# Twenty-four 64x64 zero products in place of five 128x128 ones at the start of an attention and gated-MLP kernel

## The chip, the core and the metric

One core of one Trainium2 chip runs the whole program. The metric is device microseconds of one execution, from the first to the last instruction of the kernel and what the runtime puts around it. The profile is of one execution, taken by the hardware profiler.

## What is computed

Eight batches of eight heads of linear attention (no softmax), then a gated MLP with a spatial gate, everything in single precision:

```python
kv = np.einsum('bhsd,bhse->bhde', k, v)          # 64x64 for each head
out = np.einsum('bhsd,bhde->bhse', q, kv)
attn = out / np.sqrt(np.mean(out * out, -1, keepdims=True) + 1e-06) * g_norm
x = attn.transpose(0, 2, 1, 3).reshape(8, 576, 512)
h = np.maximum(x @ w_in, 0.0)                    # 512 -> 1024
u, v = h[..., :512], h[..., 512:]
v_n = (v - mean(v)) / np.sqrt(var(v) + 1e-06)
v_s = np.einsum('ts,bsd->btd', w_spatial, v_n) + b_spatial[None, :, None]
return (u * v_s) @ w_out
```

There are 576 positions, heads of 64, and inputs in HBM.

## The kernel before

TensorE does nearly all of the arithmetic. The large products (lines 482, 515, 763) split each operand into a high and a low half of type f32r and use three matmuls for one product. The attention products (line 289 for K'V, line 320 for Q times K'V) work on 64x64 pieces in plain f32. The trace shows a plain f32 product as two matmuls, each with its own weight load, and an f32r product or a transpose as one.

Batch 0 is staged by hand, since weights and inputs arrive while it runs. The string PLAN lists its steps in program order, one token a step. Of the tokens that matter here: `L` issues the next load of keys, values or queries (lines 213 to 223, on SP's queue), `W` the next load of weights, `Kbp` the K'V products of batch b and head pair p (line 289, the result copied to KVB by ScalarE on line 305), `A` the products with Q (line 320), `D` the squares and sums for the norm (lines 365 to 373 on ScalarE, 366 on VectorE, then 232), `B` the scaling (line 390), `T` the transposes (line 425) and their split into X0H and X0L (lines 246, 247), `c` and `C` the decoding of a weight tile (lines 907 on ScalarE, 913 and 914 on VectorE), `X` its split (518, 519), `H` the products of X with the weights. Two buffers hold keys and values, so the third load of them waits for the first K'V products.

Two tokens compute nothing that is used. `N8` calls `warm(8)`, eight 128x128 products of a block of zeros (KVO) into the tile psw, line 1017. `n1` calls `filler(1)`, one such product into psh, line 1021. They keep TensorE busy while the first loads are under way.

The order in which each engine issues its instructions is not the program's. ORDER holds, for each engine, a run-length list: each number says how many of the instructions still left to pass over before the next is taken, and a number after a point how many are taken in a row. The end of the program adds dependencies that hold the scheduler to this order. On TensorE the eight products of `warm` stand in three places: one, then four, then three after the first Q products.

Of the kernel before, what the change touches and what calls it, by code (L numbers as in the profile page):

```python
# [16 lines left out]
B, H, S, D = 8, 8, 576, 64  # L17
# [15 lines left out]
ODD = 32  # L33
NB = B
PLAN = """
L L N8 n1 n1 n1 n1 W G K00 n1 n1 L L W c A00 n1 n1 n1 n1 n1 D00 C X0 B00 K01 L L W T00 c A01 D01 H00 H20 H10 H30 C X1 K02 L L W B01 T01 c A02 D02 H01 H21 H11 H31
C X2 K03 L W W B02 T02 c W A03 D03 H02 H22 H12 H32 C X3 W B03 c T03 W a0 C X4 H03 e0 H23 e2 H33 e3 H13 e1 b0 t0 c u00 C X5
L L K10 f2 F1 c u01 F0 L L W y0 F3 C X6 u02 y2 y1 W c K12 L a1 C X7 u03 b1 Z L L y3 t1 u10 A10 D10 W W E1 L L E0
u11 W z u12 h B10 A12 u13 W s T10 D12 s s s B12 T12 s s s s Y1 Y0 P Q0 O0 Q1 W p O1 R
# [1 line left out]

ORDER = {
    "PE": """
# [97 lines left out]
def body(ctx: ExitStack, tc, qT, qtl, kvm, kvt, g2, w_in, wsT, bsp, w_out, out):  # L141
    nc = tc.nc
# [10 lines left out]
    def persistent(shape, dt, name):  # L153
        return const.tile(shape, dt, name=name, tag=name)
# [36 lines left out]
    KVO = [persistent([P, 2, P], F32, f"KVO{i}") for i in range(2)]  # L191
# [76 lines left out]
    def two_banks(name):  # L268
        ps = ps_att.tile([P, 1024], F32, name=name, tag="att")
        banks = [ps[:, 0:512], ps[:, 512:1024]]  # L270
        whole[id(banks)] = ps
        return banks
# [740 lines left out]
    def warm(n):  # L1013

        ps = two_banks("psw")[0]
        for _ in range(n):
            nc.tensor.matmul(ps[:, 0:P], KVO[1][:, 1], KVO[1][:, 1], start=True, stop=True)

    def filler(n):
        for _ in range(n):  # L1020
            nc.tensor.matmul(psv[3][:, 0:P], KVO[1][:, 1], KVO[1][:, 1], start=True, stop=True)  # L1021
# [47 lines left out]
    def to_out():  # L1069
# [14 lines left out]
    two = lambda b, p: (p, p + 1) if b else (p,)  # L1084
    do = {
        "N": warm, "n": filler,
        "L": lambda: ahead(), "W": lambda: loads.pop(0)(), "c": lambda: weight64_a(makes[0].pop(0)),
        "C": lambda: weight64_b(makes[1].pop(0)),
# [86 lines left out]
    for name, text in ORDER.items():  # L1175
        left, last = queues[getattr(mybir.EngineType, name)], None
        for token in text.split():
            at, n = (int(x) for x in (token + ".1").split(".")[:2])
# [55 lines left out]
```

## Time and profile before

| | us |
|---|---|
| median of 3 runs | 475.3 |
| lowest and highest | 474.8, 475.54 |
| the profiled execution | 475.17 |
| its span, first to last instruction | 473.4 |
| TensorE matmul busy in the span | 465.7 |
| ScalarE busy | 303.2 |
| VectorE busy | 361.7 |

The profiled execution took 475.17 us, of which its span is 473.4; the other 1.8 us lie around the span. In the views, a row with a line number names the engine, the line of the kernel, the operation, the tile written and the tiles read, the shape, and how often. "idle before <-X" is the time in which the engine had nothing to do before the row, and what ended it; "issue" stands where nothing that the profile shows ended it. Matmul ends are modelled, so the distance between starts tells more than the durations.

### The profile page before, as it was taken

To read this page: it belongs to the slowest core of one execution; us is meant where nothing else is said; L and a number is where in the kernel's file an instruction comes from. 1 tells how busy PE (TensorE), PEld (TensorE's weight loads), DVE (VectorE), ACT (ScalarE), POOL (GpSimd) and SP (SyncE) were. 2 spreads that over 40 slices of the span, in tenths; PEclk is the share of its full clock that TensorE was granted. 3 is DMA by queue.
4 is the path that set the end of the run, shared out by engine and by line. 5 is a ranking of instruction groups with operands and counts; after the bars stand their busy time and mean duration, and the time that the engine had idled before them with its cause. 6 is when DMAs were issued, how large, how long until landed. Compare 5 with 4: busy or idle time off the path is not lost.

```text
span 473.4 us, 12500 instructions
## 1 busy us (share of the span) xinstructions
PE 465.7 (98%) x4922; PEld 415.5 (88%) x4922; DVE 361.7 (76%) x1007; ACT 303.2 (64%) x971; POOL 20.9 (4%) x43
## 2 busy tenths in 40 slices
PE   8999999999999999999999999899999999999996
PEld 8679998989888999889988899789998899989995
DVE  2987798876977889778866798579887679878760
ACT  4899967756546866478534886367743688547531
POOL 3000100000001010000000010000000001000000
PEclk9999999999999999999999999999999999999999
DMA  8997227226724931462713817055531344114313
GB/s 272 373 326 242 75 75 247 81 101 182 263 95 121 320 132 48 135 225 93 256 30 91 265 54 289 4 187 178 198 140 56 74 162 140 40 67 157 125 55 111
DMA packets 27763, 72.02 MB, mean 152 GB/s; under 512 B 3508, under 2 KB 8120, under 8 KB 26168
## 3 DMA queue, kind: packets, MB, share of 16 engines
q1 hardware_dynamic: 23880, 48.61, 30.9%
q0 software_dynamic: 3456, 22.02, 13.7%
q8 instruction: 38, 0.62, 0.5%
q10 hardware_dynamic: 368, 0.59, 0.4%
q14 instruction: 21, 0.17, 0.1%
HBM read 58.10 MB, written 13.11 MB: 150 GB/s over the span
## 4 chain that ended last, share of the span: by engine, by line
PE 95%; ACT 3%; issue 1%; DVE 0%; ACTq 0%
PE pso L482 21%; PE psh L515 16%; PE psb L763 10%; PE psub L763 8%; PE psa L763 5%; PE psc L763 5%; PE psuc L763 4%; PE pskv L289 4%; PE pso L320 3%; PE psu L482 3%; PE psu L763 3%; PE psua L763 2%; PE pstr L425 2%; PE psh L482 2%; PE psh L1021 1%; PE psh L763 1%
## 5 line engine op out<-in xcount | busy, mean ns | idle before, releaser
L482 PE MATMUL pso<-WO,G 128*128 128x512 f32 x384 | 110.7, 393 | 0.0
L482 PEld LDWEIGHTS pso<-WO,G 128*128 128x128 f32 x384 | 70.3, 188 | 13.1 <-ACT o L860 0.2
L515 PE MATMUL psh<-WVH,XL 128*128 128x512 f32 x112 | 43.2, 392 | 0.0
L515 PE MATMUL psh<-WVL,XH 128*128 128x512 f32 x112 | 43.1, 391 | 0.0
L515 PE MATMUL psh<-WVH,XH 128*128 128x512 f32 x112 | 43.0, 391 | 0.0
L518 ACT CAST G<-g 128x288 fp32r<-128x288 f32 (+1 forms) x56 | 22.5, 406 | 29.1 <-DVE g L782 29.0
L860 ACT COPY o<-pso 128x512 f32<-128x512 f32 x35 | 20.2, 586 | 26.9 <-PE pso L482 26.4
L494 DVE BATCH_NORM_STATS2 s<-v 128x6 f32<-128x512 f32 x31 | 21.4, 690 | 16.9 <-ACT v L488 16.4
L763 PE MATMUL psb<-WSL,VH 128*128 128x288 f32 x112 | 32.5, 296 | 0.0
L763 PE MATMUL psb<-WSH,VH 128*128 128x288 f32 x112 | 32.2, 299 | 0.0
L763 PE MATMUL psb<-WSH,VL 128*128 128x288 f32 x112 | 32.1, 295 | 0.0
L519 DVE TENSOR_TENSOR VL<-v,VH 128x512 fp32r<-128x512 f32 (+1 forms) x42 | 24.9, 599 | 8.2 <-ACT VH L518 8.1
L488 ACT ACTIVATE v<-psh 128x512 f32<-128x512 f32 x31 | 18.6, 600 | 19.6 <-PE psh L515 19.2
L519 DVE TENSOR_TENSOR G<-g,G 128x288 fp32r<-128x288 f32 (+1 forms) x56 | 23.3, 421 | 8.3 <-ACT G L518 7.5
L502 ACT ACTIVATE v<-v,mv,rv 128x512 f32<-128x512 f32 x28 | 22.6, 815 | 8.1 <-DVE mv L501 7.8
L518 ACT CAST VH<-v 128x512 fp32r<-128x512 f32 (+1 forms) x42 | 22.8, 546 | 4.7 <-DVE v L547 4.2
L515 PEld LDWEIGHTS psh<-WVH,XL 128*128 128x128 f32 x112 | 21.0, 188 | 3.8
L515 PEld LDWEIGHTS psh<-WVL,XH 128*128 128x128 f32 x112 | 21.0, 188 | 3.7
L515 PEld LDWEIGHTS psh<-WVH,XH 128*128 128x128 f32 x112 | 21.0, 188 | 3.7
L246 ACT ACTIVATE XH<-pstr,gcol 128x512 fp32r<-128x512 f32 x28 | 19.2, 689 | 6.3 <-PE pstr L425 3.9
L289 PEld LDWEIGHTS pskv<-KV 64*64 64x64 f32 (+1 forms) x960 | 18.3, 135 | 4.0 <-issue 1.7
L247 DVE SCALAR_TENSOR_TENSOR XL<-pstr,gcol,XH 128x512 fp32r<-128x512 f32 x28 | 20.6, 746 | 1.4 <-ACT XH L246 1.2
(289 smaller groups left out, 1392.7 us busy)
## 6 DMA issues: line engine op xcount, KB each, us to landing
KV<-kvm SPq DMA_DIRECT2D x32, 512.0 KB, 5.7
WO<-spare_o POOLq DMA_DIRECT2D x12, 1024.0 KB, 6.9
UX<-spare_u POOLq DMA_DIRECT2D x12, 768.0 KB, 6.8
qt<-qT SPq DMA_DIRECT2D x32, 256.0 KB, 4.4
out<-o SPq DMA_DIRECT2D x32, 256.0 KB, 3.1
stage<-w_in SPq DMA_DIRECT2D x7, 512.0 KB, 6.8
stage<-w_out SPq DMA_DIRECT2D x4, 512.0 KB, 4.1
spare_o<-WO SPq DMA_DIRECT2D x8, 256.0 KB, 4.0
```

What stands on the lines that cost most here:

```text
L246: nc.scalar.activation(hi, ps, AF.Copy, scale=gcol)
L247: nc.vector.scalar_tensor_tensor(lo, ps, gcol, f32(hi), op0=ALU.mult, op1=ALU.subtract)
L289: return nc.tensor.matmul(banks[r if b else 0][h:h + D, at:at + D], of[own, 0, h:h + D], of[own, 1, h:h + D], start=begin, stop=end)
L482: nc.tensor.matmul(ps, lt, rh, start=i == 0, stop=i == n - 1)
L488: nc.scalar.activation(v, ps, AF.Relu)
L494: nc.vector.bn_stats(s6, v)
L502: nc.scalar.activation(v, v, AF.Identity, bias=m, scale=r)
L515: nc.tensor.matmul(ps, lt, rh, start=k == 0 and i == 0, stop=k == NP - 1 and i == 2)
L518: nc.scalar.copy(hi, x)
L519: nc.vector.tensor_tensor(lo, x, f32(hi), op=ALU.subtract)
L763: nc.tensor.matmul(ps, lt, rh, start=start and i == 0, stop=stop and i == len(pairs) - 1, skip_group_check=True)
L860: nc.scalar.copy(o, ps)
```

## The change

`warm(n)` now issues n products of 128x128 and then 8n products of 64x64 of the same zeros, on rows and columns 0 to 63. PLAN calls it with 3 where it called it with 8. So three large products stay, and 24 small ones stand for the other five.

```diff
-L L N8 n1 n1 n1 n1 W G K00 n1 n1 L L W c A00 n1 n1 n1 n1 n1 D00 C X0 B00 K01 ...
+L L N3 n1 n1 n1 n1 W G K00 n1 n1 L L W c A00 n1 n1 n1 n1 n1 D00 C X0 B00 K01 ...
...
     "PE": """
-8 0 7.3 0.4 13.2 3.10 19 3.16 0.6 1.10 0 8.16 0.8 12.10 0.3 6 0 5 14.16 ...
+27 0 26.3 0.26 10.2 0.10 16 0.19 1.10 0 8.16 0.8 12.10 0.3 6 0 5 14.16 ...
...
         for _ in range(n):
             nc.tensor.matmul(ps[:, 0:P], KVO[1][:, 1], KVO[1][:, 1], start=True, stop=True)
+        for _ in range(8 * n):
+            nc.tensor.matmul(ps[0:D, 0:D], KVO[1][0:D, 1, 0:D], KVO[1][0:D, 1, 0:D], start=True, stop=True)
```

P is 128 and D is 64. The rest of the TensorE list and the lists of the other engines are as they were.

On TensorE, from the first instruction to the Q products of the second head pair, this stood before (psw and psh take the zeros of KVO; pskv takes the attention products of KV, its tail KT, and of the queries qt):

```order
L1021 MATMUL psh<-KVO_102 128x128
L1017 MATMUL psw<-KVO_102 128x128
L1021 MATMUL psh<-KVO_102 128x128 x3
L1017 MATMUL psw<-KVO_102 128x128 x4
L1021 MATMUL psh<-KVO_102 128x128 x2
L289 MATMUL pskv<-KV_103 64x64 x8
L289 MATMUL pskv<-KT_105 64x64 x2
L1021 MATMUL psh<-KVO_102 128x128
L320 MATMUL pskv<-KVB,qt 64x64 x16
L1017 MATMUL psw<-KVO_102 128x128 x3
L1021 MATMUL psh<-KVO_102 128x128 x3
L289 MATMUL pskv<-KV_104 64x64 x8
```

The two added lines make line 1021 line 1023 and put the small products on line 1019. On the same stretch stands now:

```order
L1023 MATMUL psh<-KVO_102 128x128
L1017 MATMUL psw<-KVO_102 128x128
L1023 MATMUL psh<-KVO_102 128x128 x3
L1017 MATMUL psw<-KVO_102 128x128 x2
L1019 MATMUL psw<-KVO_102 64x64 x24
L1023 MATMUL psh<-KVO_102 128x128 x2
L289 MATMUL pskv<-KV_103 64x64 x8
L289 MATMUL pskv<-KT_105 64x64 x2
L1023 MATMUL psh<-KVO_102 128x128
L320 MATMUL pskv<-KVB,qt 64x64 x16
L1023 MATMUL psh<-KVO_102 128x128 x3
L289 MATMUL pskv<-KV_104 64x64 x8
```

All 24 small products stand ahead of the first K'V products, where two large ones went; the three large ones between the first Q products and the second K'V products are gone. From there on TensorE issues the same instructions in the same order as before.

## Rows read from the trace of the kernel before

**Rows 1.** The page: engines, granted clock, instruction queue (packets, MB, share).
```profile
PE 465.7 (98%) x4922; PEld 415.5 (88%) x4922; DVE 361.7 (76%) x1007; ACT 303.2 (64%) x971; POOL 20.9 (4%) x43
...
PEclk9999999999999999999999999999999999999999
...
q8 instruction: 38, 0.62, 0.5%
```

**Rows 2.** Timeline of TensorE, first 12 us: start us, us, engine, line, what.
```profile
3.36 1.91 PE L1017 MATMUL psw<-KVO 128*128 128x128 f32 x8
5.07 1.06 PE L1021 MATMUL psh<-KVO 128*128 128x128 f32 x4
6.06 0.69 PE L289 MATMUL pskv<-KV 128*64 128x64 f32 x16
...
7.35 0.69 PE L320 MATMUL pskv<-KVB,qt 64*64 64x64 f32 x32
7.98 0.94 PE L1017 MATMUL psw<-KVO 128*128 128x128 f32 x6
8.75 0.83 PE L1021 MATMUL psh<-KVO 128*128 128x128 f32 x6
9.64 0.69 PE L289 MATMUL pskv<-KV 128*64 128x64 f32 x16
```

**Rows 3.** Timeline of ScalarE, 7 to 11 us.
```profile
7.05 0.21 ACT L305 COPY KVB<-pskv 128x64 f32<-128x64 f32 x1 [3.11 <-PE pskv L289]
...
9.19 0.69 ACT L907 ACTIVATE t<-stage 128x512 f32<-128x512 f32 x1
...
10.11 0.30 ACT L232 ACTIVATE s<-s,epsc 128x8 f32<-128x8 f32 x1
```

**Rows 4.** Waits of SP, 0 to 14 us: total us, times, longest.
```profile
SPq L213 <- PE pskv L289: 2.5, 2, 2.0
```

**Rows 5.** Windows: us, each engine's busy us and count, PEclk, DMA share, GB/s.
```profile
8.00:34.00 26.00, 24.58 (x354) 18.29 (x351) 21.81 (x56) 23.04 (x87) 0.00 (x0) 1.00 1.02 346
34.00:60.00 26.00, 26.00 (x381) 24.24 (x380) 20.90 (x65) 24.75 (x106) 3.05 (x5) 1.00 0.50 166
```

**Rows 6.** Waits by who waited for whom, 5 to 34 us.
```profile
DVE stage L913 <- DMA stage<-w_in: 8.2, 1, 8.2
...
PEld psu L763 <- ACT psh L598: 1.0, 1, 1.0
```

**Rows 7.** Timeline of TensorE, 294.7 to 299.3 us.
```profile
295.85 0.87 PE L320 MATMUL pso<-KVB,qt 64*64 64x64 f32 x45
297.95 0.56 PE L320 MATMUL pso<-KVB,qt 64*64 64x64 f32 x19 [1.24 <-issue]
```

**Rows 8.** DMA from 292.9 to 296 us: busy tenths in 40 slices, then the instruction queue.
```profile
DMA  1101010101010100000000000000000000080000
...
q8 instruction: 1, 0.02, 2.1%
```

**Rows 9.** The same from 295.6 to 300 us.
```profile
DMA  5000000000020000000000000000000050000000
...
q8 instruction: 2, 0.03, 3.0%
```

**Rows 10.** Windows: two blocks of 256 instructions as they lie before.
```profile
75.89:78.79 2.90, 2.90 (x129) 2.46 (x127) 2.70 (x9) 1.88 (x5) 0.00 (x0) 1.00 0.54 145
293.21:297.95 4.74, 3.50 (x130) 3.20 (x128) 4.46 (x11) 1.74 (x5) 0.00 (x0) 1.00 0.03 10
```

**Rows 11.** Windows: blocks as the change would cut them, in times of before.
```profile
289.62:295.87 6.25, 6.25 (x128) 5.97 (x131) 5.59 (x13) 4.43 (x10) 0.00 (x0) 1.00 0.54 186
...
207.52:213.48 5.96, 5.96 (x145) 5.61 (x138) 3.89 (x10) 4.44 (x16) 0.26 (x1) 1.00 0.97 328
151.48:153.73 2.25, 2.25 (x138) 2.18 (x137) 2.22 (x6) 2.18 (x7) 1.20 (x2) 1.00 0.28 46
```

**Rows 12.** Window just ahead of the third of these.
```profile
150.00:151.40 1.40, 1.40 (x11) 0.89 (x9) 1.37 (x3) 1.39 (x4) 0.00 (x0) 1.00 0.85 187
```

More of the change, by code (lines that the diff above doesn't have):

```diff
@@ L35 @@
 PLAN = """
-L L N8 n1 n1 n1 n1 W G K00 n1 n1 L L W c A00 n1 n1 n1 n1 n1 D00 C X0 B00 K01 L L W T00 c A01 D01 H00 H20 H10 H30 C X1 K02 L L W B01 T01 c A02 D02 H01 H21 H11 H31
+L L N3 n1 n1 n1 n1 W G K00 n1 n1 L L W c A00 n1 n1 n1 n1 n1 D00 C X0 B00 K01 L L W T00 c A01 D01 H00 H20 H10 H30 C X1 K02 L L W B01 T01 c A02 D02 H01 H21 H11 H31
 C X2 K03 L W W B02 T02 c W A03 D03 H02 H22 H12 H32 C X3 W B03 c T03 W a0 C X4 H03 e0 H23 e2 H33 e3 H13 e1 b0 t0 c u00 C X5
```

2 rows, old and new, of the table ORDER are left out of this document.

## The prediction

> **What bounds the kernel now.** I read the page first. TensorE is busy for 465.7 of 473.4 us, so what it loses or gains is the time of the kernel [rows 1]. Its matmuls and weight loads make 9,844 instructions, and the instruction queue moved 38 packets of together 0.62 MB: some 16 KB or 256 instructions each. So TensorE's code comes in blocks of about 256 instructions, and the change puts every later instruction at another place in its block.
>
> Then the timeline of the first microseconds. TensorE runs zero products from 1.06 us until the first K'V products begin at 6.06, with no wait named before them [rows 2]: the zeros themselves set when the real work starts. The clock shows in the starts: eight matmuls of 128 columns take 5.07 - 3.36 = 1.71 us, 0.214 each, while six of the same take 8.75 - 7.98 = 0.77 us later on, 0.13 each and near 0.11 once running. The page prints the full clock in all slices [rows 1], but these spacings are those of the lower level (1.2 GHz) before 6.06 us and of the upper (2.4 GHz) after, following five microseconds of unbroken 128x128 products.
>
> Next, the windows. From 8 to 34 us all share the load: TensorE is busy for 24.58 of 26 us, ScalarE for 23.04, the DMA engines throughout (share 1.02). From 34 to 60 TensorE is busy for 26.00 of 26 [rows 5]. So a delay that is still there at 34 us stays to the end. Before that, TensorE has 1.42 us of idle time in which one could be lost; its last wait of that stage is for ScalarE [rows 6].
>
> Last, the one long gap of TensorE: at 297.95 us, in the middle of the 64 matmuls of one Q step, it stands idle for 1.24 us, put down to "issue", with no semaphore [rows 7]. An instruction packet came in slice 36 of 40 between 292.9 and 296, that is near 295.7, and the next in slice 33 between 295.6 and 300, near 299.1 to 299.2 [rows 8, 9]. A block that came late fits both: the packet of 295.7 carried the missing block, which was usable 2.3 us after the packet's start, and the first instruction of it let the next packet be asked for, which came 1.2 us later. I take the stalled instruction as the first of a block and count off 256 either way. The block before it then lies from 293.21 to 297.95, with 3.50 us of work [rows 10]. Another lies from 75.89 to 78.79, 2.90 us without a gap: dense code alone does not stall, the packet must come late too.
>
> **The change, part by part.**
>
> *Two large products leave their place, 24 small ones come in.* The small ones begin after four matmuls of the eight, at 3.36 + 4 x 0.214 = 4.22 us. They are 48 matmuls, all on the same 64x64 corner of the array, so I expect them one after another. With 64 columns instead of 128 one costs half of 0.214, thus 0.107 us, at the lower clock. At the upper, half of 0.11 is 0.056, and the first K'V row gives (0.69 - 0.23) / 7 = 0.066 a step for its pairs; I take 0.06. If the clock rises near 6.06 as before, 17 are done by then, and the other 31 last 1.86 us, to 7.92. The four filler matmuls behind them take 0.55 at the upper clock, and 0.13 pass before the first K'V start as they do now. K'V starts at 8.6 us instead of 6.06: **+2.5 us**. Lower bound: if they overlapped as 32 Q matmuls on four corners do (7.98 - 7.35 = 0.63 us, 0.02 each, 0.04 at the lower clock), they would last 1.9 us and the fillers 0.85 more, +1.0. Upper bound: all of it at the lower clock, 48 x 0.107 + 4 x 0.214 = 6.0 us from 4.22, +4.3. I take the middle, since nothing in the same corner is seen to overlap.
>
> *Three large products after the first Q step go.* That frees 0.77 us [rows 2], which counts only if TensorE is what the second K'V step waits for. Today it starts at 9.64. In the changed kernel it starts near 11.3 (8.6, plus 7.98 - 6.06 up to the end of Q, plus 0.8 for the remaining fillers), +1.7. But the norm of the first head pair runs through ScalarE: copy at 7.05, then 10.11 for the root [rows 3], all behind the first K'V, and the later transposes need it. Only its wait for a weight tile (9.19; VectorE waited 8.2 us for the same load [rows 6]) gets shorter, by some 0.2. That path is late by 2.3 us, and it is the later of the two. So the 0.77 count for nothing; if the second K'V decided, the shift would be 1.7.
>
> *What is queued behind.* SP's third load of keys waits up to 2.0 us for the first K'V products [rows 4], and the weight and query loads stand behind it on the same queue. They go out about 2.5 us later, the DMA engines fall idle for about as long, and this delays no one more than the shift itself does. Of 2.5 us, I carry **+2.2** past 34 us. Bounds: 2.5 less all of TensorE's idle time (1.42) is 1.1 below; above, 2.5. I stay near the upper end because the idle times are waits for ScalarE and VectorE work that hangs on the same first products, so they move along.
>
> *The code moves in its blocks.* 24 small products bring 48 matmuls and 48 loads, five large ones took 10 and 10: the stream is 76 instructions longer, and each block boundary falls 76 instructions earlier in the work, 0.3 of a block. The boundary at 297.95 moves to 295.87, and the block that ends there lasts 6.25 us instead of 3.50 [rows 11]: its packet has time. **-1.24 us.** Two new blocks are tight. One holds K'V and Q alone, 2.25 us, and the DMA share just before it is 0.85 [rows 12]; its packet takes 3.5 us if it goes as after the gap (1.2 to start, 2.3 to be usable), so asked for when the block begins, it is 1.3 us late, and asked for 1.3 us earlier, as code taken in ahead of its execution would be, it is in time: 0 to 1.3. The other lasts 5.96 us under a DMA share of 0.97. The late packet came 2.5 us after its block began and was usable 2.3 later, 4.8 together; allowing 2 us more for the load gives 0 to 0.8. I take **+0.4** for both, with 0 and 2.1 as ends, since other dense blocks pass without a gap [rows 10].
>
> The Trainium skill (Runtime: NRT & Kernel Launch, section Instruction fetch mechanics) says that TensorE holds 2,048 instructions and that the cost of crossing into a new block is mostly hidden. By that, moving the boundaries is worth nothing and the sum would be +2.2 us alone. The trace speaks against it in one place only: the gap of 1.24 us between two instructions that wait for nothing [rows 7].
>
> **Sum.** +2.2 - 1.24 + 0.4 = +1.36 us on 475.17, thus 476.5 us. The profiled execution lies 0.13 below the median of the runs (475.3), which I leave as it is.
>
> **The rivals.**
>
> *The start is absorbed (faster).* DMA is full from 8 to 34 us. If weights, not the first products, are what ScalarE runs short of, a start 2.5 us later is lost in waits and the block gain remains: 475.17 - 1.24 + 0.2 = 474.1. For it: the share of 1.02 [rows 5]. Against: the only wait for a weight load ends at 9.19 [rows 3, 6]. Decided by whether ScalarE's work from 20 us on starts at its old times.
>
> *The clock rises later (slower).* Small products fill a quarter of the array, and before the rise TensorE had run only full ones. If full ones up to 4.22 us and small ones after that do not bring the rise near 6.06, all of the zeros run at the lower clock: K'V at 10.4, +4.3, of which 4.1 are kept: 475.17 + 4.1 - 1.24 + 0.4 = 478.4. Decided by whether starts of small matmuls after 6.1 us are 0.107 or 0.06 apart.
>
> *The gap at 297.95 is not one of blocks, or one of the same size opens elsewhere (slower).* Then 475.17 + 2.2 = 477.4. For it: only one such gap exists among 38 packets. Against: it fits the packets before and after it [rows 8, 9]. This is also the time that the rule of the Trainium skill would give.
>
> *The small products overlap.* Start +1.0, of it 0.9 kept: 475.17 + 0.9 - 1.24 + 0.2 = 475.0, no change.
>
> **How the numbers follow.** 0.2% is 0.95 us, about what a measurement of this kernel can tell: below 474.35 is faster, above 476.25 slower. Forecast 0.47, its own range 475.6 to 477.4 by the shift (1.7 to 2.5) and the new blocks (0 to 1); 0.3 of it is slower, 0.17 the same. Absorbed 0.16, of it 0.13 faster and 0.03 the same. Later clock 0.16, slower. Blocks worth nothing 0.12, of it 0.1 slower and 0.02 the same. Overlap 0.09, the same or, for 0.03 of it, faster. That gives faster 0.16, same 0.28, slower 0.56. The range from 474.0 to 478.5 leaves out the later half of a late clock and the lower end of the absorbed case.
>
> **What would show it.** Right: line 1019's matmuls 0.107 us apart and then near 0.06; the first K'V at about 8.6; the third load of keys issued about 2.5 us later than now; from 34 us on everything later by 2.2; no gap in the Q step near 300 us; at most short "issue" gaps near 156 and 215.7 (153.73 and 213.48 plus 2.2). Wrong: first K'V before 7 or after 10; a work item of 60 us onward that is not later by 1.6 to 2.5; a gap over 1 us in another K'V or Q step.

## The result, and the profile after

The changed kernel takes 477.45 us (median of 20 runs, 475.66 to 481.39), the kernel before on the same chip 475.36 (20 runs, 473.49 to 476.32). The ratio is 1.0063, with a 95% interval of 1.0044 to 1.0083: slower by 0.6%.

The 20 runs of the changed kernel are not one heap. Eleven lie from 475.66 to 477.83 (median 476.52), nine from 479.85 to 481.39 (median 480.84), and none between. The median of all 20 lies in the hole between the two. What parts them is the main thing that the experiments had to find. I call them the lower and the upper group; the expectations quoted below call them the earlier and the later one.

The execution that was profiled first took 477.83 us, the top of the lower group. Its page:

```profile
span 476.1 us, 12577 instructions
...
PE 467.1 (98%) x4960; PEld 416.2 (87%) x4960; DVE 361.9 (76%) x1007; ACT 303.1 (64%) x971; POOL 20.9 (4%) x43
...
q8 instruction: 39, 0.64, 0.6%
```

TensorE has 38 matmuls and 38 loads more, and one instruction packet more, as counted [rows 1]. Its busy time rose by 1.4 us and the span by 2.7, so 1.3 us came as idle time, although the idle time of 1.24 near 298 us [rows 7] should be gone by the theory of blocks. The timeline of TensorE from 4 us, and its Q step near 300 us:

```profile
4.35 3.06 PE L1019 MATMUL psw<-KVO 64*64 64x64 f32 x48
7.34 0.71 PE L1023 MATMUL psh<-KVO 128*128 128x128 f32 x4
7.98 0.69 PE L289 MATMUL pskv<-KV 128*64 128x64 f32 x16
...
9.28 0.69 PE L320 MATMUL pskv<-KVB,qt 64*64 64x64 f32 x32
...
10.77 0.69 PE L289 MATMUL pskv<-KV 128*64 128x64 f32 x16
...
300.10 1.14 PE L320 MATMUL pso<-KVB,qt 64*64 64x64 f32 x64
301.18 0.40 PE L763 MATMUL psb<-WSH,VH 128*128 128x288 f32 x1
```

Beside [rows 2, 7] this says three things. The first K'V products start 1.92 us later (7.98 for 6.06). The Q step that started at 295.85 starts at 300.10, so 4.25 us of delay have gathered by then, more than twice the delay of the start. And the idle time of 1.24 us in that step is gone: all 64 matmuls follow one another. What this is worth to the kernel is read from products on both sides of it, first of the kernel before, then of the changed one:

```profile
294.00 0.29 PE L771 MATMUL psc<-WTL,TB 128*128 128x288 f32 x1
...
298.44 0.40 PE L763 MATMUL psb<-WSH,VH 128*128 128x288 f32 x1
...
301.58 0.29 PE L769 MATMUL psb<-WTH,TA 128*128 128x288 f32 x1
```

```profile
298.02 0.29 PE L771 MATMUL psc<-WTL,TB 128*128 128x288 f32 x1
...
304.36 0.30 PE L769 MATMUL psb<-WTH,TA 128*128 128x288 f32 x1
```

From its first matmul to the product behind it (298.44 before, 301.18 now) the step is 1.51 us shorter, but TensorE waits 0.2 us more just ahead of it and gives up a little behind it. The delay is 4.02 us ahead of the step (298.02 for 294.00) and 2.78 behind it (304.36 for 301.58): 1.24 us stay.

Where the second half of the delay came from is seen in SP's timeline, before and after, and in the waits of the changed kernel between 0 and 40 us:

```profile
6.78 0.33 SPq L213 DMA_DIRECT2D KV<-kvm  x1
...
7.70 0.58 SPq L881 DMA_DIRECT2D stage<-w_in  x1
```

```profile
8.71 0.33 SPq L213 DMA_DIRECT2D KV<-kvm  x1
9.08 1.73 SPq L215 DMA_DIRECT2D KT<-kvt  x1
10.86 0.58 SPq L881 DMA_DIRECT2D stage<-w_in  x1
```

```profile
PEld psh L763 <- ACT X0H L246: 2.5, 3, 1.7
ACT t L907 <- DMA stage<-w_in: 1.6, 2, 1.1
...
PEld pskv L289 <- DMA KT<-kvt: 0.9, 1, 0.9
```

The third load of keys is issued at 8.71, where the kernel before issued it at 6.78, and the weight load behind it at 10.86 for 7.70. While SP waited, the DMA engines ran dry. The windows of the changed kernel, to be read against the share of 1.02 in [rows 5]:

```profile
8.00:10.00 2.00, 2.00 (x56) 1.68 (x55) 0.43 (x1) 0.21 (x1) 0.00 (x0) 1.00 0.52 120
10.00:12.00 2.00, 2.00 (x28) 1.68 (x28) 0.79 (x2) 1.93 (x11) 0.00 (x0) 1.00 0.71 269
```

ScalarE then waits twice for a weight tile, TensorE once for a tail of keys, and once 1.27 us (at 21.07) for ScalarE's line 246, which stands on ScalarE right behind the late tile of 19.75. The delay grows from 1.92 to 4.06 us, as the product of psu shows that TensorE starts when ScalarE's line 598 is done, before and after:

```profile
33.40 0.40 PE L763 MATMUL psu<-X0H,WUH 128*128 128x288 f32 x1 [0.75 <-ACT psh L598]
```

```profile
37.46 0.40 PE L763 MATMUL psu<-X0H,WUH 128*128 128x288 f32 x1 [0.74 <-ACT psh L598]
```

Three more profiles of the changed kernel, taken later, show how it varies. "Kept" is the delay at that product of psu:

| execution | time | first K'V | delay | kept | Q step starts | gap in it |
|---|---|---|---|---|---|---|
| before | 475.17 | 6.06 | | | 295.85 | 1.24 |
| changed, 1st | 477.83 | 7.98 | 1.92 | 4.06 | 300.10 | none |
| changed, 2nd | 476.26 | 7.93 | 1.87 | 2.43 | 298.32 | none |
| changed, 3rd | 477.20 | 8.44 | 2.38 | 2.82 | 299.33 | none |
| changed, 4th | 481.25 | 10.81 | 4.75 | 7.25 | 303.42 | none |

The fourth is of the upper group. In the second the DMA engines ran dry in the same way (share 0.71 from 8 to 10 us), and yet 0.6 us and not 2.1 came on top of the start. So the late loads are seen as waits in the first execution, but that the dry stretch alone makes them late is not shown.

### The profile page after: what moved, and what is told of

Its sections match the earlier page's. It is cut to its first block, busy times and chain, and to the rows that moved or that the text cites. A ratio compares the mean times of both kernels' runs of the same rounds, so it can differ in the third digit from the quotient of the medians.

```text
span 476.1 us, 12577 instructions
## 1 busy us (share of the span) xinstructions
PE 467.1 (98%) x4960; PEld 416.2 (87%) x4960; DVE 361.9 (76%) x1007; ACT 303.1 (64%) x971; POOL 20.9 (4%) x43
## 4 chain that ended last, share of the span: by engine, by line
PE 93%; ACT 3%; DMA 2%; DVE 1%; issue 0%; SPq 0%; ACTq 0%
PE pso L482 21%; PE psh L515 16%; PE psb L763 9%; PE psub L763 8%; PE psa L763 5%; PE psc L763 5%; PE psuc L763 4%; PE pskv L289 4%; PE pso L320 3%; PE psu L482 3%; PE psu L763 3%; DMA stage<-w_in 2%; PE psua L763 2%; PE pstr L425 2%; PE psh L482 2%; PE psc L771 1%
## 5 line engine op out<-in xcount | busy, mean ns | idle before, releaser
L247 DVE SCALAR_TENSOR_TENSOR XL<-pstr,gcol,XH 128x512 fp32r<-128x512 f32 x28 | 20.6, 744 | 1.4 <-ACT XH L246 1.2
```

The lines of the kernel that those rows point to most:

```text
L247: nc.vector.scalar_tensor_tensor(lo, ps, gcol, f32(hi), op0=ALU.mult, op1=ALU.subtract)
```

## The experiments

The theory at their start: the change costs by its later first products, gains by its blocks, and the upper group is made by TensorE's clock. The rivals: the moved blocks cost time elsewhere, the loads do it, or the upper group is a disturbance that has nothing to do with the small products.

**The changed kernel again, unchanged, for its profile.** Three runs.

> The changed kernel once more, as it is, for one profile. If it falls in the group of 475.7 to 477.8: clock up near 4.5 us as in the first profile. If in the group of 479.9 to 481.4: by the theory of a late rise of the clock, the first K'V rows at 1.12 instead of 0.69 us and the kept shift near 8; by its rival (the same clock, a stall elsewhere), first K'V as in the first profile and an idle time of 3 us or more at another place.

> The changed kernel once more, as it is, for one profile, in the hope of an execution of the later group. Later group, 479.9 to 481.4: starts of the 64x64 products 0.11 apart to the last, first K'V near 10.5 in 1.12 us, kept shift near 6.2, as in the run with the other order of loads. Earlier group, 475.7 to 477.8: first K'V near 7.9, kept shift 2 to 4.

> The changed kernel a fourth time, as it is, for one profile of the later group if it falls there. Later group, 479.9 to 481.4: starts of the 64x64 products 0.11 apart to the last, first K'V near 10.5 in 1.12 us, kept shift near 6.2. Earlier group, 475.7 to 477.8: small products from 0.11 to 0.06 apart, first K'V between 7.9 and 8.5, kept shift 2 to 4.

The second and third executions fell in the lower group (476.26 and 477.20), the fourth in the upper (481.25). Of the second and the third, the small products and the first K'V:

```profile
4.35 3.01 PE L1019 MATMUL psw<-KVO 64*64 64x64 f32 x48
...
7.93 0.69 PE L289 MATMUL pskv<-KV 128*64 128x64 f32 x16
```

```profile
4.35 3.52 PE L1019 MATMUL psw<-KVO 64*64 64x64 f32 x48
...
8.44 0.69 PE L289 MATMUL pskv<-KV 128*64 128x64 f32 x16
```

Of the fourth:

```profile
4.35 5.38 PE L1019 MATMUL psw<-KVO 64*64 64x64 f32 x48
9.66 1.22 PE L1023 MATMUL psh<-KVO 128*128 128x128 f32 x4
10.81 1.12 PE L289 MATMUL pskv<-KV 128*64 128x64 f32 x16
...
13.00 1.13 PE L320 MATMUL pskv<-KVB,qt 64*64 64x64 f32 x32
...
19.51 1.12 PE L289 MATMUL pskv<-KV 128*64 128x64 f32 x16
20.56 0.37 PE L289 MATMUL pskv<-KT 64*64 64x64 f32 x4
...
26.30 0.69 PE L289 MATMUL pskv<-KV 128*64 128x64 f32 x16
```

The starts are (9.66 - 4.35) / 48 = 0.111 us apart here and (7.29 - 4.35) / 48 = 0.061 in the second execution, the two levels of the clock. In the fourth the lower level lasts until about 20.6 us: K'V and Q rows take 1.12 and 1.13 us, and only from the row of 20.56 on the time of before (0.69 in [rows 2]). So the upper group is one of a late clock, in the changed kernel itself. It costs twice: 4.75 us to the first K'V, then 2.5 more until 20 us (7.25 kept), while the K'V, Q and filler products also ran at half speed. Less the 1.24 of the gap that is 6.01, against 6.08 measured (481.25 - 475.17).

**The same time in front without small products.** The kernel before, with 256 columns in each of the first five large products: the start is delayed, no instruction is added, the array stays full.

```diff
-        for _ in range(n):
-            nc.tensor.matmul(ps[:, 0:P], KVO[1][:, 1], KVO[1][:, 1], start=True, stop=True)
+        for i in range(n):
+            w = 2 * P if i < 5 else P
+            nc.tensor.matmul(ps[:, 0:w], KVO[1][:, 1], ..., start=True, stop=True)
```

> The kernel before with the first five zero products 256 columns wide instead of 128: same count of instructions, so same blocks, but a later first K'V step. Theory A: the first K'V starts near 7.5 to 8.2 us, the gap of 1.2 us in the Q step near 298 us (plus the shift) is still there, and the time is 2 to 4 us above the kernel before, 477.5 to 479.5 us. Rival B (the start does not matter): within 0.5 us of the kernel before. Rival C: the runs stay in one group, since all zero products fill the array.

Its first K'V starts at 7.85, 1.79 us late. Its ten runs are one group, 474.04 to 476.92 (median 476.65), at a ratio of 1.0008 (0.9992 to 1.0024): the delay of the start alone makes no upper group. The expected 477.5 to 479.5 us did not come, and by the times alone the rival, that the start does not matter, is not ruled out. The profile says why so little is left: of the 1.79 us, 1.67 are kept at the product of psu (35.07), and the gap of the Q step was missing in this execution of 476.73 us, though not one instruction had moved in its block:

```profile
298.82 1.14 PE L320 MATMUL pso<-KVB,qt 64*64 64x64 f32 x64
```

Its instruction packet came near 295.8, 3.1 us before the step, where in the kernel before it came with the start of the step [rows 7, 8]. So the gap goes with a packet that comes late, and with these blocks it does so in some executions and not in others. What makes it late in one and not in the other stays open.

**Smaller products.** The changed kernel with 32x32 products of 4 columns for the 64x64 ones.

```diff
-            nc.tensor.matmul(ps[0:D, 0:D], KVO[1][0:D, 1, 0:D], KVO[1][0:D, 1, 0:D], ...)
+            nc.tensor.matmul(ps[0:32, 0:4], KVO[1][0:32, 1, 0:32], KVO[1][0:32, 1, 0:4], ...)
```

> The 24 small products keep their place and their 96 instructions but work on a 32x32 corner and 4 columns. Theory A (the change loses time because its zeros last longer and hold up the first K'V step, and gains 1.24 us because the block boundaries move): the small products last under 2 us, the first K'V starts between 5.5 and 6.5 us, the gap in the Q step near 298 us is gone, and the time falls below the kernel before by about 1.2 us, to 474.0 to 474.8 us. Rival B (the later start costs nothing that the boundaries do not explain: new block stalls make the kernel slower): the time stays near that of the changed kernel, 476 us or more, since the instructions lie in the same blocks. Rival C (a weak start of TensorE delays the rise of its clock): the K'V and Q matmuls after 6 us run at half speed in some executions and the runs fall into two groups some 3 to 4 us apart.

```profile
4.35 2.72 PE L1019 MATMUL psw<-KVO 32*32 32x4 f32 x48
7.00 1.22 PE L1023 MATMUL psh<-KVO 128*128 128x128 f32 x4
8.15 1.12 PE L289 MATMUL pskv<-KV 128*64 128x64 f32 x16
```

The tiny products last 2.65 us and not under 2. The first K'V of this execution starts at 8.15, close to the lower group of the changed kernel, and yet it took 480.26 us: at 8.15 the clock was still at its lower level (1.12 us a row). The median of its nine executions is 480.26, the ratio 1.0064 (1.0032 to 1.0097); five lie at 480.3 to 480.6, two at 477.5 and 478.0, two at 474.9 and 475.0. The last two lie below the 475.76 of the kernel before beside it, where an early clock and the gain of the blocks would put them; neither was profiled. A short start does not help where the clock stays down.

**Full-array products in the same number.** The 24 products with a 128x128 weight and 64 columns.

```diff
-            nc.tensor.matmul(ps[0:D, 0:D], KVO[1][0:D, 1, 0:D], KVO[1][0:D, 1, 0:D], ...)
+            nc.tensor.matmul(ps[:, 0:D], KVO[1][:, 1], KVO[1][:, 1, 0:D], ...)
```

> The changed kernel with its 24 products on all 128 rows and columns of the stationary operand and 64 columns moving: the same length each at the same clock, the same blocks, but a full array. Theory A with C (the second group of slow executions of the changed kernel comes from the clock, which rises late when a quarter of the array is filled): the runs fall into one group, 475.5 to 477.5 us, first K'V near 8 us, no gap near 300 us. Rival (the two groups have another cause, for instance the loads): two groups again, 476 and 480 to 481 us.

This did not hold the cost of the start fixed, and so answers little. The 48 matmuls lasted from 4.21 to 14.34, 0.211 each, as long as with 128 columns. At this lower level a matmul thus takes 0.21 us with a weight of 128 columns, whether 128 or 64 columns pass over it, 0.111 with one of 64 and 0.055 with one of 32 (the tiny products above): the size of the weight sets the pace. The first K'V starts at 15.44 in 1.12 us, so in this execution the clock was still down behind 48 products with a full weight and few columns. The median is 484.43 (ratio 1.0151, 1.0105 to 1.0198), but the six runs are not the one group that was expected: four lie from 484.42 to 485.20, two at 478.57 and 479.93. These two were not profiled; an earlier rise of the clock would fit them.

**One whole block more.** 69 tiny products in the place of the 24, so that 256 instructions more than in the kernel before stand ahead and every block lies as it did before.

```diff
-        for _ in range(8 * n):
-            nc.tensor.matmul(ps[0:D, 0:D], KVO[1][0:D, 1, 0:D], KVO[1][0:D, 1, 0:D], ...)
+        for _ in range(23 * n):
+            nc.tensor.matmul(ps[0:32, 0:4], KVO[1][0:32, 1, 0:32], KVO[1][0:32, 1, 0:4], ...)
```

> 69 of the tiny products of e1 in place of five large ones: 256 instructions more than the kernel before, so every later instruction lies at its old place in a block of 256. Theory A (the gap comes from a block that is fetched late): the gap of about 1.2 us returns in the same Q step, after 45 of its 64 matmuls, near 298 us plus the shift of the start. Rival (the gap is not one of blocks, or the block is not 256 instructions): no gap there, as in the changed kernel. The start is 1.5 to 4 us later than before, so the time is 476 to 481 us.

```profile
305.10 0.90 PE L320 MATMUL pso<-KVB,qt 64*64 64x64 f32 x44
307.26 0.56 PE L320 MATMUL pso<-KVB,qt 64*64 64x64 f32 x20 [1.26 <-issue]
```

The gap is back, in the same step and within one matmul of the same place (after 44 of 64, 45 before), as long as before [rows 7]. Its packet came near 305.0, again with the start of the step, and the stalled matmul 2.2 us after it, where it was 2.3 before. All eleven profiles whose boundaries lay 76 or 40 instructions earlier (four of the changed kernel, and those of the other kernels above and below) show the step without a gap. So the gap goes with the place in the block: two of three profiles with the old places have it, none of the eleven with others, and it came back where it was expected. That the block has 256 instructions and not a part of that rests on the count of packets [rows 1]. The one run took 484.69 us, more than the 476 to 481 expected, with tiny products unbroken from 4.35 to 11.79 and a first K'V at 12.95 in 1.12 us: behind 7.4 us of them the clock was still at its lower level.

**The loads.** The changed kernel with the second weight load ahead of the third load of keys on SP's queue.

```diff
     "SP": """
-0.5 1.2 0.4 1 0.2 24 0 1 22 0 4 ...
+0.11 1 0.2 24 0 1 22 0 4 ...
```

> The changed kernel, with the second load of w_in ahead of the third load of keys on SP's queue, so that it no longer waits behind SP's wait for the first K'V products. Theory (of the 4.06 us that the change keeps past 40 us, 1.9 come from the start and 2.1 from loads that stood behind that wait): DMA share between 8 and 10 us back above 0.8, the w_in tile lands some 2 us earlier, kept shift in an execution with an early rise of the clock down to 2 to 3 us, its times 474.7 to 476; the executions with a late rise of the clock stay, at 478.5 to 480.5. Rival (the loads are not what holds ScalarE): times as the changed kernel, 475.7 to 477.8 and 479.9 to 481.4.

Twelve runs, six from 476.06 to 476.88 and six from 480.03 to 480.53, ratio 1.0053 (1.0028 to 1.0079). The load goes out at 5.08 us, and the DMA share from 8 to 10 us is 0.97, as expected, but then 0.10 from 10 to 12, where the fourth execution above had 0.46 and 0.00 (both profiles are of the upper group): the dry stretch came later and was not filled. The lower group's median is 476.41 against 476.52: the order of these two loads moves the time by nothing that can be told. So the rival holds for this load. Which load makes the kept delay of the lower group run from 2.4 to 4.1 us stays open.

**Full products first.** The changed kernel with the four fillers, 128x128 products, ahead of the 24 small ones.

```diff
     "PE": """
-27 0 26.3 0.26 10.2 0.10 16 0.19 1.10 ...
+27 0 26.3 0.2 34.2 0.24 0.10 16 0.19 1.10 ...
```

> The changed kernel with the four filler matmuls of 128x128 ahead of the 24 small products instead of behind them; same instructions, same number, same blocks after. Theory (the late group of times is a late rise of the clock, decided by how long full products have run before the small ones begin): unbroken full products now to 5.07 instead of 4.21, so the share of executions above 479 falls from 9 of 20 to 5 or fewer, and the median to 476.0 to 477. Rival (the late group has another cause, or only the small products' number counts): 7 to 11 of 20 above 479, median 476.5 to 480.5.

```profile
4.21 0.69 PE L1023 MATMUL psh<-KVO 128*128 128x128 f32 x4
4.83 3.01 PE L1019 MATMUL psw<-KVO 64*64 64x64 f32 x48
7.76 0.69 PE L289 MATMUL pskv<-KV 128*64 128x64 f32 x16
```

One of twelve runs lies above 479 (480.83), where the changed kernel with either order of loads had 15 of 32. Median 476.83, ratio 1.0019 (0.9999 to 1.0040). The same products in the same number, in another order, and the upper group nearly goes, as the theory expected: in the profiled execution the full products run to 4.83 before the small ones begin, and not to 4.35. It is one order in twelve runs (chance alone would give so few in some 3 of 100 cases), so that it is the length of their stretch, and not another effect of the order, is not shown. In the profiled execution the clock rose before 4.83 already (four matmuls of 128 columns in 0.62 us, 0.155 each).

**The blocks without the delay.** All five large products back in front, and 22 tiny ones in place of the three late large ones: 76 instructions more, as in the change.

```diff
-        for _ in range(n):
+        for _ in range(5):
             nc.tensor.matmul(ps[:, 0:P], KVO[1][:, 1], KVO[1][:, 1], start=True, stop=True)
+        for _ in range(22):
+            nc.tensor.matmul(ps[0:32, 0:4], KVO[1][0:32, 1, 0:32], KVO[1][0:32, 1, 0:4], ...)
```

> All five large products of before stay ahead of the first K'V products, and 22 tiny products (32x32 stationary, 4 columns) stand for the three later large ones: 76 more instructions, as in the change, so that every later block boundary lies where the change puts it, but nothing stands longer before the first K'V. Theory (the change costs by its later start and, in some executions, by a later rise of the clock; its blocks are a gain): first K'V at 6.06 as before, clock up at the same time as before in all executions, no issue gap near 298 to 302; median 474.0 to 475.2, one group of times. Rival (moved blocks are themselves what costs): 476 to 477.5 as the change. Rival 2 (tiny products let the clock fall back): K'V rows of the second head pair at 1.12 instead of 0.69 us, 478 or more.

> The kernel with 22 tiny products after the first Q step once more, to narrow its interval: by the theory that its blocks are a gain and its times of 476.9 to 479.1 (4 of 12) executions with a late rise of the clock, again two groups, the lower one at 473.7 to 475.2 with 12 or more of 20. By the rival that those four were a disturbance of that chip: one group, 20 of 20 below 475.5.

The two runs of it gave 474.65 and 474.67 us (ratios 0.9996, 0.9971 to 1.0022, and 0.9991, 0.9968 to 1.0013). Of 24 executions 17 lie from 473.75 to 475.57, and 7 from 476.92 to 479.05. One of the latter was profiled (478.39): first K'V at 6.05 as before, no gap in the Q step, but

```profile
8.32 1.55 PE L1019 MATMUL psw<-KVO 32*32 32x4 f32 x44
9.80 1.25 PE L1023 MATMUL psh<-KVO 128*128 128x128 f32 x6
10.98 1.12 PE L289 MATMUL pskv<-KV 128*64 128x64 f32 x16
```

```profile
4.00:8.00 4.00, 4.00 (x52) 3.52 (x55) 0.43 (x1) 0.21 (x1) 0.52 (x2) 1.00 1.04 352
8.00:12.00 4.00, 4.00 (x94) 3.61 (x84) 2.22 (x7) 2.05 (x11) 0.00 (x0) 0.78 0.98 332
...
16.00:20.00 4.00, 4.00 (x42) 2.85 (x42) 2.80 (x8) 2.11 (x10) 0.00 (x0) 0.50 0.85 279
20.00:24.00 4.00, 4.00 (x49) 2.69 (x42) 2.64 (x7) 3.15 (x13) 0.00 (x0) 0.94 0.82 273
```

The clock column (the third from the end) shows it outright: TensorE was at its upper level, ran the tiny products, and fell to 0.50 until shortly after 20 us. This holds for the whole group: the mean granted clock of its 7 executions is 0.987 to 0.991, that of the other 17 is 0.995 to 1.0. So the second rival of this experiment holds in part of its executions: the clock can also fall again behind small products. In the other executions the time is that of a gain by the blocks, though the intervals of all the runs together show none.

**Fewer of them, behind the clock.** All five large products in front and two of the three late ones kept; 12 tiny products, 40 instructions net, in place of the filler between the second K'V and Q products.

```diff
-L L N8 n1 n1 n1 n1 W G K00 n1 n1 L L W c A00 n1 n1 n1 n1 n1 D00 ...
+L L N7 n1 n1 n1 n1 W G K00 n1 n1 L L W c A00 n1 n1 n1 n1 m D00 ...
...
+    def tiny():
+        for _ in range(12):
+            nc.tensor.matmul(psv[3][0:32, 0:4], KVO[1][0:32, 1, 0:32], KVO[1][0:32, 1, 0:4], ...)
```

> As before, with all five large products in front, but one of the three late large ones and the filler between the second K'V and Q products gone, and 12 tiny products (32x32 stationary, 4 columns) in that filler's place, near 10.7 us: 40 more instructions, boundaries 40 earlier. At the 0.034 us a matmul of the run with tiny products after the first Q step they take 0.82 us where 0.47 went. Theory (moving the block boundary out of the Q step near 298 is the gain, and small products cost only where they stand before the clock has risen): no issue gap near 298, at most 0.35 us kept from the start, median 474.2 to 475.2, no execution above 477. Rival (the gap moves along with any boundary): median within 0.3 of before. Rival 2 (times above 477 come from something else, as they also do in some executions of the kernel before): as many above 477 as the kernel before has.

```profile
6.06 0.83 PE L289 MATMUL pskv<-KV 128*64 128x64 f32 x16
...
10.31 0.92 PE L1025 MATMUL psh<-KVO 32*32 32x4 f32 x24
11.16 0.69 PE L320 MATMUL pskv<-KVB,qt 64*64 64x64 f32 x32
...
33.36 0.40 PE L763 MATMUL psu<-X0H,WUH 128*128 128x288 f32 x1 [0.77 <-ACT psh L598]
...
296.05 1.14 PE L320 MATMUL pso<-KVB,qt 64*64 64x64 f32 x64
```

The median is 473.93 us (7 runs, 473.36 to 474.80) beside 475.46 of the kernel before (18 runs), ratio 0.9958 (0.9942 to 0.9974). It beats both kernels, and lies a little below the 474.2 to 475.2 expected. The second Q step starts 0.22 us later than before (11.16 for 10.94), and by 33.4 us nothing of that is left. The gap is gone. In the profile the product of 294.00 is 0.18 us late (294.18), that of 301.58 comes 1.05 us early (300.53): the block term, with next to nothing paid for it. No run is above 477, but 7 runs beside 2 of 18 of the kernel before do not tell the second rival's theory from the first.

## Why the prediction was right, and where it was not

The forecast of 476.5 us meets the lower group (median 476.52), and its sign comes from the mechanisms that it named: a later start that is kept, and a gap that goes. That it meets the group so closely is partly luck: the start was less late than forecast, more of it was kept, and the 0.4 us for new gaps never came. That the median of all runs is 477.45 comes from the rival with the late clock, to which it gave 0.16 and which came in 9 of 20 runs; the forecast's own range ended at 477.4. Two of its signs of being wrong came too: the work past 60 us was later by more than 2.5 us in three of the four executions, and the fourth had its first K'V after 10 us.

*Two large products go, 24 small ones come.* Right, when the clock is said with it. The small products were put at 0.107 us at the lower clock and 0.06 at the upper; they measure 0.111 and 0.061. The reason given for the half, 64 columns instead of 128, was not the right one: with 64 columns and a full weight a product took 0.211, so it is the smaller weight. The sum of 8.6 for the first K'V assumed a rise near 6.06. The third execution has 8.44, with the rise in the midst of its small products (0.072 us apart on the mean), the first two have 7.98 and 7.93, with nearly all of them at the upper level. The moment of the rise is not the kernel's alone. The kernel with 22 late tiny products is the same as the one before up to the first K'V, and that started at 5.40 in one execution and 6.05 in another. The Trainium skill (TensorE: Matmul & The Clock Gate, section What's actually happening) says that this moment differs from run to run of one kernel; these traces agree, with 5.40 and 6.05.

*Three large products behind the first Q step go.* Right that they count for little. The second K'V started 1.13 us later than before (10.77 for 9.64) in the first execution, so 0.8 of its 1.92 was won there; but the transposes behind the norm started 1.7 us later.

*What is queued behind.* This is the step that failed in size: "Of 2.5 us, I carry +2.2". The lower group kept 2.43, 2.82 and 4.06 of 1.87, 2.38 and 1.92. The delay grew where I let it shrink. I had written that the late loads delay "no one more than the shift itself does". In the first execution they did: ScalarE waited 1.6 us for weight tiles, and TensorE 0.9 for a tail of keys. The DMA engines were full from 8 to 34 us before [rows 5] and moved little at 8 to 10 us now (share 0.52), and it is near at hand that this made the loads late. But it is not shown: the wide products, with a start 1.79 us late and a share of 0.70 there, kept 1.67, and the load that was moved ahead changed nothing. Nor did the idle time of TensorE take up the delay: its longest piece, the wait for ScalarE's line 598, stood at 0.75 in the kernel before and at 0.74 to 0.75 in all four executions of the changed one.

*The code moves in its blocks.* Right in place, sign and size: I put 1.24 us, and across the Q step the delay fell by 1.24 in the first execution (4.02 to 2.78). The two tight blocks cost nothing: no "issue" gap opens near 156 or 216 in any of the four executions, where I put +0.4. What I had not seen is that the gap does not come in every execution even with the blocks of the kernel before, as the run with wide products showed. Three of the 18 runs of the kernel before beside the last experiments lie at or below 474.75, where a run without the gap would lie; that these are such runs is only argued. The rule of the Trainium skill (Runtime: NRT & Kernel Launch, section Instruction fetch mechanics), that a crossing is mostly hidden, agrees with this trace for all but one of the 38 packets of the kernel before: no other idle time over 0.1 us ahead of a matmul is put down to "issue". That one cost 1.24 us.

*The late clock.* The condition was right ("if full ones up to 4.22 us and small ones after that do not bring the rise near 6.06"), and the price too low: 478.4 for 480.84. I carried the lower level to the end of the zeros only. In the fourth execution it lasted to about 20.6 us, through the K'V and Q products of 64x64 pieces (to about 16.4 in the profile with the other order of loads), and this added 2.5 us. The chance was too low as well: the full products ran unbroken for five microseconds before (1.06 to 6.06), and the change lets them run for 3.3 only (1.06 to 4.35) before the small ones begin.

*The start is absorbed.* It did not happen: ScalarE's work from 20 us on ran late with the rest. Its copy of 20.05 (line 305) came at 23.83 in the first execution and at 21.77 in the second.

## What to carry to other kernels

Full products that only keep TensorE busy until its clock has risen are not to be exchanged for small ones: here the exchange went with a slower group of 9 in 20 executions, in which the one profiled had the clock down until about 20 us, and with small ones soon after the rise the level was lost again in 7 of 24. Where the DMA engines are full, do not count on a later start being absorbed, nor on its staying as it is: of 1.8 to 1.9 us at the start, 1.7 to 4.1 were kept. If a gap of about a microsecond stands between two instructions that wait for nothing, count the instructions from it in 256s, and move the boundary by a few tiny products at a place that has slack: here 12 of them were worth 0.4%.

## What the runs showed of the hardware that was not expected

- The clock column shows 1.00 from the start of the execution in every profile, also where the starts are those of the lower level (3 to 6 us of the kernel before, 8 to 16 us of the fourth execution). It did show the later fall to 0.50. The first rise was read from the spacing of the starts alone.
- Tiny products (32x32, 4 columns) cost 0.055 us a matmul at the lower level ((7.00 - 4.35) / 48) and 0.035 at the upper ((11.16 - 10.31) / 24), however little they compute.
- With a full 128x128 weight, 64 columns cost as much as 128 at the lower level (0.211 and 0.214 us); with weights of 64 and 32 columns the spacing is a half and a quarter of that (0.111 and 0.055).
- The kernel before has itself some runs up to 478.9 us beside the experiments. Of its 68 runs there, nine lie above 477, all with a mean granted clock of 0.994 to 0.996; all the others but one (476.4 us) have 0.998 or more. So they too lost the upper level for a while. No profile here caught one, so where and behind which products stays open.
